# Attention and routed experts on one core: the rows of the first and last pair of batches turned by VectorE in squares of 32 instead of by TensorE

## The chip, the cores and the metric

The kernel runs on one core of one Trainium2 chip. The metric is the device time of one execution in microseconds. A core has TensorE (PE; its weight loads are shown apart as PEld), VectorE (DVE), ScalarE (ACT), GpSimd (POOL) and SyncE (SP), each with its own queue of instructions in program order, and 16 DMA engines that all queues share.

## The reference

Two blocks, one behind the other. First attention with a linear bias, a causal window of 128 and a softmax; then a gate picks one of eight experts for each token, and the token's row goes through that expert's two matrices and is scaled by the gate's probability.

```python
# q, k, v: (8 batches, 8 heads, 576 positions, 64), float32
scores = q @ k.T / sqrt(64)
rel = pos[:, None] - pos[None, :]
scores = where((rel >= 0) & (rel < 128), scores - slope[h] * abs(rel), -1e9)
x = softmax(scores) @ v               # -> rows of tokens: (4608, 512)

logits = x @ w_gate                   # (4608, 8)
expert = argmax(logits, 1)
gate = softmax(logits)[expert]
y = relu(x @ w1[expert]) @ w2[expert] # w1: (8, 512, 1024), w2: (8, 1024, 512)
out = gate[:, None] * y
```

## The kernel before

**Attention.** Batches are taken in four pairs (`bp` 0 to 3), and a pair in four units of two heads (`u` 0 to 15). A unit is worked in four steps, so a loop of 64 iterations (`i = 4 * u + g`) carries the attention. In iteration i TensorE makes the scores of iteration i+2 (`scores`, L756), ACT takes their exponential (L762), VectorE multiplies them by the bias factors (L765, L770), and TensorE multiplies the probabilities of iteration i by the values (`values`, L791). `finish` copies the sum of a half unit to `xT` by ACT, adds up the softmax's denominators by TensorE (L823) and adds them to `sumT` by VectorE (L834). So `xT` holds the attention's result of a pair with features on partitions and tokens along the columns, not yet divided.

**Loads.** SP issues them: `load_part` in iteration i loads a quarter of unit u+2, the keys at g = 0, the queries at g = 1, the values of one batch at g = 2 and of the other at g = 3. Ahead of each stands a copy of four bytes, `no_earlier_than` (L636), that waits for the multiplied probabilities of iteration i+1. The values of units 6 and 7 are the exception: POOL issues those, and nothing holds them back but their buffer, of which there are three. In units 5 and 6 SP also loads quarters of the first expert's first matrix (L561).

**Rows.** When a pair is done, its rows must go to the DRAM tensor `x_rows`, token by token, so that the experts can gather them. A pair has nine tiles of 128 tokens (`t` 0 to 8; tile 8 holds 64 tokens of each batch). `row_turned` turns a tile by four TensorE transposes into a PSUM tile `m` (L1007), and ACT copies it to a tile `xs` (L1009). `row_out` has POOL put the row's scales `es` into the last columns (L1016) and store the row by one DMA (L1021). A row in `x_rows` is four pieces of 132 numbers: 32 features of each of four head pairs, and four scales. There are four `xs` tiles in turn (pool `rows`), and two PSUM tiles `m`, which the row transposes share with `finish`, `gate`, `turn`, `place` and `enlist`.

**Order of the work behind a pair.** The order is written by hand. For each pair the gate's logits (`gate`, `turn`), the scales (`scale_a`, `scale_b`, `scale_c`; the last gives `es`), the place of each token in its expert's list (`count`, `place`, `ones_at`, `enlist`) and the nine rows are cut into tasks. `behind(bp)` lists 16 for pairs 0 and 1, and one is taken at the end of each iteration of the next pair (at g = 2 in its middle). For pair 0 these are iterations 16 to 31; rows 0 and 1 are turned in iterations 21 and 23, `scale_c`, `count` and the first two stores lie in iteration 24, and rows 2 to 8 in iterations 25, 26, 27, 29, 30 and 31. Pair 3 has no attention behind it: `with_tail` lists 14 tasks, and `strassen1` of the first expert takes one after each of its 14 groups of matmuls.

**Experts.** An expert's first 512 tokens go through both layers with seven half-size products instead of eight (`strassen1`, L1357; `strassen2`, L1414); the sums that this needs are VectorE's (L529 to L532 and L537 to L540). Tokens beyond 512 go through small plain groups (L1453, L1469). The first two experts gather whole rows, which TensorE turns (L1177); all others gather by pieces into squares of 32, which VectorE turns (`to_columns`, L1180). The constant `to_squares` holds four 0/1 matrices that carry a number per token to the place where its squares lie; `pieces` uses it for the indices (L1056). The second expert's weights take the memory of the pools that hold `xT` and `xs`, so their load waits until those are done with (`end_of_tail`).

Of the kernel before, what the change touches and what calls it, by code (L numbers as in the profile page):

```python
# [8 lines left out]
F32 = mybir.dt.float32  # L9
# [6 lines left out]
P = 128  # L16
# [441 lines left out]
def kernel(  # L458
# [12 lines left out]
    nc = tc.nc  # L471
# [8 lines left out]
    HP = H // 2  # L480
    KB = P // 2
# [24 lines left out]
    with ExitStack() as fast:  # L506
# [99 lines left out]
        def load_v(u, b, eng, k0=0, k1=NK):  # L606
            bp, hp = units[u]
            if u not in v_sb:
                v_sb[u] = vp.tile([P, NK, P], F32, name="v_sb")
            eng.dma_start(  # L610
                v_sb[u][b * KB : (b + 1) * KB, k0:k1, :], v4[2 * bp + b, :, k0:k1, hp * P : (hp + 1) * P],
            )
# [391 lines left out]
        def row_turned(bp, t):  # L1004
            ps = ps_m.tile([P, 512], F32, name="m")
            for hp in range(HP):
                nc.tensor.transpose(ps[:, hp * P : (hp + 1) * P], xT[bp][:, hp, t * P : (t + 1) * P], ident[:])  # L1007
            xs = xs_of[bp, t] = rows.tile([P, NA, PW], F32, name="xs")
            nc.scalar.copy(  # L1009
                xs[:, :, :PD].rearrange("p a (h f) -> p h a f", h=HP), ps.rearrange("p (h a f) -> p h a f", h=HP, a=NA),  # L1010
            )

        def row_out(bp, t):

            xs = xs_of.pop((bp, t))
            nc.gpsimd.tensor_copy(  # L1016
                xs[:, :, PD:].rearrange("p (r x) h -> p r x h", r=2),
                es_of[bp][:, t].unsqueeze(2).to_broadcast([P, 2, 2, HP]),
            )
            for p0, n, r0 in placed(bp, t):  # L1020
                nc.gpsimd.dma_start(x_d[r0 : r0 + n, :], xs[p0 : p0 + n].rearrange("p a w -> p (a w)"))  # L1021

        def row(bp, t):
            row_turned(bp, t)
            row_out(bp, t)


        NC = E * NJ + XU
        g_idx = rte.tile([P, NR * NJ], I32, name="g_idx")
        p_idx = rte.tile([P, NC - NR * NJ, NA], I32, name="p_idx")  # L1030
# [479 lines left out]
        def with_tail(g, w2s):  # L1510

            bp = BP - 1
            rs = [lambda t=t: row(bp, t) for t in range(TPB)]
            early = [lambda t=t: row_turned(bp, t) for t in range(3)]
            w = [[f] for f in w2s]
            a, b, c, n, p, o, e = (
                [lambda f=f: f(bp)] for f in (scale_a, scale_b, scale_c, count, place, ones_at, enlist)
            )
# [81 lines left out]
```

## Time and profile before

| | us |
|---|---|
| median of 3 runs | 687.96 |
| the three runs | 686.35, 687.96, 689.75 |
| the profiled execution | 687.13 |
| its span, first to last instruction | 685.4 |
| TensorE busy in it | 663.6 |
| VectorE, ACT, POOL busy | 366.9, 208.3, 229.8 |
| attention, about | 0 to 177 |
| first expert's first layer with pair 3's tasks, about | 177 to 213 |
| all other experts' work, about | 213 to 685 |

The page gives busy times for each engine, and a chain: the work that ended last, followed back from the last instruction. A group of instructions is one line: line of the kernel, engine, operation, tile written and tiles read, shape, count, then busy time and the mean time of one in ns, then the engine's idle time just before them and what ended it. Views by stretch give the busy time of every engine between two moments, the clock granted to TensorE (1.00 is full speed) and the DMA engines' share. All times are microseconds from the span's start.

### The profile page before, as it was taken

The page shows a single profiled execution, that of the slowest core. Times are in us where ns is not written, and L with a number is a line of the kernel's source. Part 1 is how long each engine was busy: PE and PEld are TensorE (multiplying, and loading weights), DVE is VectorE, ACT ScalarE, POOL GpSimd, SP SyncE. Part 2 cuts the span into 40 slices and gives each one's busy share as a digit, 9 for nine tenths or more (in the row PEclk, how much of TensorE's full clock was granted, in tenths as well). Part 3 has the DMA queues.
Part 4 walks back from the last instruction along what each step waited for, and adds up shares of the span by engine and source line. Part 5 has one row for each costly group of instructions (what it writes and reads, how often), then busy time and mean ns, then how long its engine had stood idle before and what let it go on. Part 6 is the DMA issues. An engine that isn't in the chain of part 4 may idle for free.

```text
span 685.4 us, 14622 instructions
## 1 busy us (share of the span) xinstructions
PE 663.6 (97%) x6096; PEld 557.5 (81%) x6096; DVE 366.9 (54%) x691; ACT 208.3 (30%) x379; POOL 229.8 (34%) x344
## 2 busy tenths in 40 slices
PE   7998998999999999999999999999999999999996
PEld 6877877787688888878897887888788878878893
DVE  4556749786469467614843563385157435633500
ACT  5655555465342223113112310231131123012210
POOL 8010412215033175217224702752272257023020
PEclk9999999999999999999999999999999999999998
DMA  8776978875428555284457328542834583294010
GB/s 261 207 207 194 296 239 241 231 236 168 138 96 318 186 185 166 62 295 143 148 183 279 85 99 290 187 163 82 298 123 142 180 280 100 80 303 158 1 61 9
DMA packets 56909, 122.00 MB, mean 178 GB/s; under 512 B 5345, under 2 KB 22529, under 8 KB 56834
## 3 DMA queue, kind: packets, MB, share of 16 engines
q1 hardware_dynamic: 44562, 89.17, 40.3%
q0 software_dynamic: 11120, 30.92, 13.6%
q8 instruction: 50, 0.82, 0.5%
q10 hardware_dynamic: 1152, 0.88, 0.4%
q14 instruction: 25, 0.20, 0.1%
HBM read 101.79 MB, written 19.96 MB: 178 GB/s over the span
## 4 chain that ended last, share of the span: by engine, by line
PE 83%; issue 9%; DVE 4%; ACT 2%; POOL 1%; DMA 1%; ACTq 0%; POOLq 0%; DVEq 0%
PE sp L756 6%; PE at L791 5%; PE pair0b L1357 5%; PE pair1b L1414 5%; PE pair1a L1414 5%; PE pair0a L1357 4%; PE pair2b L1357 4%; PE pair0a L1414 4%; PE pair2a L1357 4%; PE pair0b L1414 4%; PE pair1b L1357 4%; PE pair2a L1414 4%; PE pair1a L1357 4%; PE pair2b L1414 4%; PE m L823 3%
## 5 line engine op out<-in xcount | busy, mean ns | idle before, releaser
L1152 POOL DMA_INDIRECT xg<-x_rows,p_idx x124 | 124.8, 1006 | 37.8 <-issue 36.9
L1437 POOL DMA_INDIRECT out_dram<-zo,s_idx x39 | 44.7, 1146 | 249.7 <-DVE zo L1428 133.4
L765 DVE TENSOR_TENSOR pe<-pe,fac 128x768 f32<-128x768 f32 x48 | 45.9, 959 | 40.2 <-ACT pe L762 40.0
L756 PE MATMUL sp<-q_sb,k_sb 64*64 64x192 f32 (+2 forms) x1152 | 59.1, 326 | 8.4 <-DMA q_sb<-in_qT_dram 4.9
L762 ACT ACTIVATE pe<-sp 128x768 f32<-128x768 f32 x64 | 51.9, 811 | 43.0 <-PE sp L756 40.4
L791 PE MATMUL at<-pe,v_sb 64*64 64x192 f32 (+2 forms) x1408 | 59.8, 290 | 0.9 <-DVE pe L765 0.7
L756 PEld LDWEIGHTS sp<-q_sb,k_sb 64*64 64x64 f32 x1152 | 42.0, 139 | 17.5 <-issue 7.3
L791 PEld LDWEIGHTS at<-pe,v_sb 64*64 64x64 f32 x1408 | 47.4, 138 | 7.1 <-issue 2.3
L1016 POOL COPY xs<-es 128x16 f32<-128x16 f32 x36 | 11.3, 314 | 82.4 <-DVE es L930 77.4
L1021 POOL DMA_DIRECT2D x_rows<-xs x40 | 21.9, 549 | 35.6 <-issue 16.3
L1368 ACT ACTIVATE h<-h 128x512 f32<-128x512 f32 x32 | 20.2, 632 | 39.5 <-DVE h L1367 39.5
L823 PE MATMUL m<-pe,ind 128*32 128x192 f32 (+2 forms) x704 | 29.5, 286 | 0.3 <-issue 0.3
L1009 ACT COPY xs<-m 128x512 f32<-128x512 f32 x36 | 20.7, 585 | 22.4 <-PE m L1007 8.0
L1164 DVE TENSOR_TENSOR xn<-xg 128x512 f32<-128x512 f32 x39 | 26.3, 676 | 0.2 <-DMA xg<-x_rows,p_idx 0.2
L823 PEld LDWEIGHTS m<-pe,ind 128*32 128x32 f32 x704 | 23.0, 109 | 2.7 <-issue 0.7
L1007 PE MATMUL m<-ident,xT 128*128 128x128 f32 x144 | 21.8, 282 | 2.1 <-DVE sumT L834 1.7
L1180 DVE STREAM_TRANSPOSE xgT<-xn 128x512 f32<-128x512 f32 x31 | 22.1, 711 | 1.1
L537 DVE TENSOR_TENSOR w2s<-w 128x512 f32<-128x512 f32 x16 | 11.0, 688 | 20.0 <-DMA w<-in_moe_w_dram 20.0
L1469 PE MATMUL pair2a<-w,h 128*128 128x512 f32 x48 | 21.1, 592 | 0.0
L1007 PEld LDWEIGHTS m<-ident,xT 128*128 128x128 f32 x144 | 15.8, 142 | 5.9 <-DVE sumT L834 2.1
L808 ACT COPY xT<-at 128x640 f32<-128x640 f32 (+1 forms) x32 | 18.7, 585 | 5.7 <-PE at L791 5.6
L770 DVE TENSOR_TENSOR pe<-pe,fac 128x768 f32<-128x768 f32 x16 | 15.3, 954 | 8.8 <-ACT pe L762 8.8
(364 smaller groups left out, 1384.8 us busy)
## 6 DMA issues: line engine op xcount, KB each, us to landing
w<-in_moe_w_dram SPq DMA_DIRECT2D x29, 2048.0 KB
k_sb<-in_kT_dram SPq DMA_DIRECT2D x15, 576.0 KB
q_sb<-in_qT_dram SPq DMA_DIRECT2D x15, 576.0 KB
x_rows<-xs POOLq DMA_DIRECT2D x32, 264.0 KB, 4.5
v_sb<-in_v_dram SPq DMA_DIRECT2D x26, 288.0 KB
w<-in_moe_w_dram SPq DMA_DIRECT2D x4, 512.0 KB
xg<-x_rows,p_idx POOLq DMA_INDIRECT x124, 2.6
v_sb<-in_v_dram POOLq DMA_DIRECT2D x4, 288.0 KB, 7.7
```

Source lines behind the costliest of these rows:

```text
L756: nc.tensor.matmul(sp[c * KB : (c + 1) * KB, r, c0 : c0 + n], lhsT=k_sb[u][hs, c, kb * KB : (kb + 1) * KB], rhs=q_sb[u][hs, c, kb * KB : k ...
L762: nc.scalar.activation(pe[:], sp[:, :, :GC], AF.Exp, scale=SCALE)
L765: nc.vector.tensor_tensor(pe.rearrange("p r (k c) -> p r k c", k=2), pe.rearrange("p r (k c) -> p r k c", k=2), fac[:, h0 : h0 + 2, None, ...
L791: nc.tensor.matmul(acc[r * D : (r + 1) * D, c, lo - q0 : hi - q0], lhsT=v_sb[u][c * KB : (c + 1) * KB, kb, r * D : (r + 1) * D], rhs=pe[c ...
L823: nc.tensor.matmul(sm[32 * j : 32 * j + 32, lo - q0 : hi - q0], lhsT=none[:] if pe is None else ind[:, hp, :], rhs=fac[:, 0, :KB] if pe is ...
L1007: nc.tensor.transpose(ps[:, hp * P : (hp + 1) * P], xT[bp][:, hp, t * P : (t + 1) * P], ident[:])
L1152: nc.gpsimd.indirect_dma_start(out=to, out_offset=None, in_=where, in_offset=bass.IndirectOffsetOnAxis(ap=idx, axis=0),)
L1164: nc.vector.tensor_tensor(xn[:], x, s.unsqueeze(3).to_broadcast([P, NA, HP, TQ]), op=ALU.mult)
L1180: nc.vector.transpose(to.rearrange("p h (k j) -> p k h j", j=TQ), xn[:])
L1357: nc.tensor.matmul(ps[:, f * 256 : (f + 1) * 256], lhsT=left[m][:, d, fb * P : (fb + 1) * P], rhs=right[m][:, d, :], start=(m in (1, 2, 5) ...
L1414: nc.tensor.matmul(ps[:, :256], lhsT=left[m][:, f, c * P : (c + 1) * P], rhs=right[m][:, f, :], start=(m in (1, 2, 5) and f == 0), stop=Tr ...
L1437: ins = nc.gpsimd.indirect_dma_start(out=out[:, :], out_offset=bass.IndirectOffsetOnAxis(ap=s_idx[:, g["c0"] + j : g["c0"] + j + 1], axis= ...
```

## The change

For pairs 0 and 3 the rows are no longer turned by TensorE. VectorE turns each 32x32 square of `xT` in place of its tile (`squares_turned`), so that in `xs` partition 32a + i holds piece a of the tokens i, 32 + i, 64 + i and 96 + i. The scales must lie on those partitions too: `scales_squared` carries `es` there by four products with `to_squares` and two ACT copies. `squares_out` puts them in by POOL and stores by pieces: one DMA for each of the four pieces (eight for tile 8), in runs of 132 numbers. Pair 0 stores from POOL, tile by tile. Pair 3 turns its tiles 0 to 7 into a spare `xT` buffer, and SP stores them in groups of four tiles, then tile 8. The rows of pairs 1 and 2 stay as they were. The values of units 6 and 7 are issued by SP like all others.

```diff
-                load_v(u, g - 2, nc.gpsimd if u in (6, 7) else nc.sync)
+                load_v(u, g - 2, nc.sync)
...
+        def scales_squared(bp):
+            ps = ps_m.tile([P, 512], F32, name="m")
+            n = TPB * H
+            for k in range(NA):
+                nc.tensor.matmul(
+                    ps[:, k * n : (k + 1) * n], lhsT=K["to_squares"][:, k, :],
+                    rhs=es_of[bp].rearrange("p t r h -> p (t r h)"), start=(k == 0), stop=True, skip_group_check=True,
+                )
+            sq = sq_of[bp] = small.tile([P, TPB, NA, HP], F32, name="sq")
+            ps5 = ps[:, : NA * n].rearrange("p (k t r h) -> p k t r h", k=NA, t=TPB, r=2)
+            for r in range(2):
+                half = slice(r * KB, (r + 1) * KB)
+                nc.scalar.copy(sq[half].rearrange("p t k h -> p k t h"), ps5[half, :, :, r, :])
+
+        def squares_turned(bp, t):
+            if bp in spare and t < TPB - 1:
+                w = NA * PW
+                flat = spare[bp].rearrange("p h n -> p (h n)")
+                xs = flat[:, t * w : (t + 1) * w].rearrange("p (k w) -> p k w", k=NA)
+            else:
+                xs = rows.tile([P, NA, PW], F32, name="xs")
+            xs_of[bp, t] = xs
+            nc.vector.transpose(
+                xs[:, :, :PD].rearrange("p k (h j) -> p k h j", h=HP),
+                xT[bp][:, :, t * P : (t + 1) * P].rearrange("p h (k i) -> p k h i", k=NA),
+            )
+
+        def squares_out(bp, t, eng, n=1):
+            for k in range(t, t + n):
+                nc.gpsimd.tensor_copy(xs_of[bp, k][:, :, PD:], sq_of[bp][:, k])
...
+            for p0, m, r0 in placed(bp, t):
+                for a in range(NA):
+                    eng.dma_start(
+                        x_d[r0 : r0 + n * m, a * PW : (a + 1) * PW].rearrange("(k i) w -> i k w", i=TQ),
+                        xs[a * TQ : (a + 1) * TQ, p0 // TQ : p0 // TQ + n * m // TQ, :],
+                    )
...
 # behind(bp)
+            if bp == 0:
+                turned = [lambda t=t: squares_turned(bp, t) for t in range(2)]
+                outs = [lambda: scales_squared(bp)] + [lambda t=t: squares_out(bp, t, nc.gpsimd) for t in range(2)]
+                rs = [
+                    lambda t=t: (squares_turned(bp, t), squares_out(bp, t, nc.gpsimd)) for t in range(TPB)
+                ]
             return [g3[0:1], g3[1:2], g3[2:] + t3[0:1], t3[1:], a, turned[0:1], b, turned[1:2], c + n + outs,
                     rs[2:3], p + rs[3:4], rs[4:5], o, rs[5:6], rs[6:7], e + rs[7:9]]
...
 # with_tail(g, w2s)
-                [lambda k=k: gate(bp, k) for k in range(3)], [lambda k=k: turn(bp, k) for k in range(3)], a, early[0:2], b,
-                early[2:3] + w[0], c + n + [lambda t=t: row_out(bp, t) for t in range(3)], rs[3:5] + w[1],
-                p + rs[5:6], rs[6:7], o, rs[7:9] + w[2], e + w[3] + w[4], [table_fixed] + w[5],
+                [lambda k=k: gate(bp, k) for k in range(3)] + rt[0:1], [lambda k=k: turn(bp, k) for k in range(3)] + rt[1:2],
+                a, rt[2:3], b, rt[3:4], c + n, rt[4:5] + w[0], q + p + ro[0:1] + rt[8:9], rt[5:6] + o, rt[6:8] + ro[2:3],
+                e + ro[1:2] + w[1], [table_fixed] + w[2], w[3] + w[4] + w[5],
```

In `with_tail`, `rt` are the nine turns, `ro` the three groups of stores, `q` is `scales_squared`, and `w` are the first expert's `w2` sums.

More of the change, by code (lines that the diff above doesn't have):

```diff
@@ L1025, in row @@
             row_out(bp, t)
+        sq_of = {}
+        spare = {}
+        def scales_squared(bp):
[26 more added lines that the diff above has]
+                nc.gpsimd.tensor_copy(xs_of[bp, k][:, :, PD:], sq_of[bp][:, k])
+            if n == 1:
+                xs = xs_of.pop((bp, t))
+            else:
+                w = NA * PW
+                flat = spare[bp].rearrange("p h n -> p (h n)")
+                xs = flat[:, t * w : (t + n) * w].rearrange("p (k w) -> p k w", k=n * NA)
+            for p0, m, r0 in placed(bp, t):
[4 more added lines that the diff above has]
+                    )
         NC = E * NJ + XU
@@ L1512, in with_tail @@
             bp = BP - 1
-            rs = [lambda t=t: row(bp, t) for t in range(TPB)]
-            early = [lambda t=t: row_turned(bp, t) for t in range(3)]
+            spare[bp] = xp.tile([P, HP, 2 * S], F32, name="xT")
+            rt = [lambda t=t: squares_turned(bp, t) for t in range(TPB)]
+            ro = [lambda: squares_out(bp, 0, nc.sync, 4), lambda: squares_out(bp, 4, nc.sync, 4), lambda: squares_out(bp, 8, nc.sync)]
             w = [[f] for f in w2s]
-            a, b, c, n, p, o, e = (
-                [lambda f=f: f(bp)] for f in (scale_a, scale_b, scale_c, count, place, ones_at, enlist)
+            a, b, c, n, q, p, o, e = (
+                [lambda f=f: f(bp)]
+                for f in (scale_a, scale_b, scale_c, count, scales_squared, place, ones_at, enlist)
             )
             todo = [
-                [lambda k=k: gate(bp, k) for k in range(3)], [lambda k=k: turn(bp, k) for k in range(3)], a, early[0:2], b,
-                early[2:3] + w[0], c + n + [lambda t=t: row_out(bp, t) for t in range(3)], rs[3:5] + w[1],
-                p + rs[5:6], rs[6:7], o, rs[7:9] + w[2], e + w[3] + w[4], [table_fixed] + w[5],
+                [lambda k=k: gate(bp, k) for k in range(3)] + rt[0:1], [lambda k=k: turn(bp, k) for k in range(3)] + rt[1:2],
+                a, rt[2:3], b, rt[3:4], c + n, rt[4:5] + w[0], q + p + ro[0:1] + rt[8:9], rt[5:6] + o, rt[6:8] + ro[2:3],
+                e + ro[1:2] + w[1], [table_fixed] + w[2], w[3] + w[4] + w[5],
             ]
```

## Prediction

> **What bounds the kernel now.** First the page's busy row, its clock row and its chain, to see which engine to count in.
>
> ```profile
> PE 663.6 (97%) x6096; PEld 557.5 (81%) x6096; DVE 366.9 (54%) x691; ACT 208.3 (30%) x379; POOL 229.8 (34%) x344
> PEclk9999999999999999999999999999999999999998
> PE 83%; issue 9%; DVE 4%; ACT 2%; POOL 1%; DMA 1%; ACTq 0%; POOLq 0%; DVEq 0%
> ```
>
> TensorE is busy for 97% of the span and is 83% of the chain, so work taken from it counts, unless another engine becomes late in that stage. Next the groups of instructions, for what a row costs.
>
> ```profile
> L1007 PE MATMUL m<-ident,xT 128*128 128x128 f32 x144 | 21.8, 282 | 2.1 <-DVE sumT L834 1.7 <-ACT xs L1009 0.4
> L1009 ACT COPY xs<-m 128x512 f32<-128x512 f32 x36 | 20.7, 585 | 22.4 <-PE m L1007 8.0 <-issue 7.1 <-POOL xs L1016 6.1
> L1180 DVE STREAM_TRANSPOSE xgT<-xn 128x512 f32<-128x512 f32 x31 | 22.1, 711 | 1.1
> L1021 POOL DMA_DIRECT2D x_rows<-xs x40 | 21.9, 549 | 35.6 <-issue 16.3 <-ACT xs L1009 12.5 <-POOL xs L1016 6.9
> L1056 PE MATMUL m<-ta,to_squares 128*128 128x24 f32 (+1 forms) x16 | 1.9, 252 | 0.0
> DMA to landing us min/median/max: 2.3/4.6/8.2
> ```
>
> (The last line is from the question about L1021: issue of a row store to its landing.) Then the busy times by stretch; columns are PE, PEld, DVE, ACT, POOL, granted clock, DMA share, GB/s.
>
> ```profile
> 52.40:56.90 4.50, 4.48 (x109) 3.75 (x108) 2.58 (x10) 3.39 (x6) 0.23 (x1) 1.00 0.88 223
> 56.90:60.30 3.40, 0.80 (x25) 0.83 (x29) 3.26 (x9) 0.02 (x1) 0.00 (x0) 1.00 0.24 74
> 60.30:63.70 3.40, 3.40 (x60) 3.36 (x56) 1.90 (x6) 1.54 (x2) 0.00 (x0) 0.50 0.69 193
> 65.00:95.00 30.00, 29.10 (x608) 22.98 (x610) 17.95 (x36) 16.50 (x28) 8.84 (x19) 1.00 0.87 279
> 177.20:213.00 35.80, 34.54 (x206) 28.80 (x205) 22.83 (x59) 14.15 (x27) 7.85 (x19) 1.00 0.44 156
> ```
>
> Last the timeline where TensorE stands still in the first pair's stage.
>
> ```profile
> 51.13 0.37 SPq L598 DMA_DIRECT2D q_sb<-in_qT_dram  x1
> 51.17 1.46 POOL L610 DMA_DIRECT2D v_sb<-in_v_dram  x2 [9.21 <-PE at L791]
> 59.50 0.72 PE L756 MATMUL sp<-q_sb,k_sb 64*64 64x192 f32 x12 [2.63 <-issue]
> ```
>
> The reader is to see one event here. Unit 6's queries (L598) and unit 7's values, which POOL issues as soon as their buffer is free, leave within 0.04 us and share the DMA engines. The queries land only at 59.4 (8.3 us; the keys just before, issued at 48.80, took 4.6), the scores of unit 6 wait 2.63 us, and the clock is half for the 3.41 us from 60.28: 2.6 + 1.7 = 4.3 us lost.
>
> **The change, part by part.** "Iteration" is a step of the attention loop, four to a unit; pair 0's row work lies in iterations 20 to 31 (52 to 88 us), pair 3's between 177 and 213.
>
> *Values of units 6, 7 to SyncE.* Four loads move behind SP's pace copies: unit 7's are issued in iterations 22 and 23 rather than at 51.17. SP's other value loads take 0.67 us of issue each, and SP is two units ahead. The queries of unit 6 then land in the 4.6 us of the keys, by about 54, before they are asked for at 56.9. The 4.3 us go. What is late next is VectorE, below.
>
> *Rows of pair 0.* Removed: 9 rows of four transposes, 0.58 us each by start to start on TensorE (74.64 to 75.22 in one row): 5.2 us, and 9 ACT copies of 0.585, which cost nothing beside 16.5 of 30 us busy. Added on VectorE: 9 transposes of the L1180 kind and size, 9 x 0.71 = 6.4 us. Added on TensorE: four products with `to_squares`, 8 instructions; L1056 has 16 in 1.9 us, so 1.0 us (72 columns against 24 is no dearer: L993's 18 with 48 columns take 2.14). ACT gets two small copies, about 0.3 us each, between its exponential of 72 elements (L924, 0.26) and its copy of 256 (L832, 0.37).
>
> The price is a wait. In the old order `es`, the last result of VectorE's scale chain, was read by POOL alone; now TensorE reads it in `scales_squared` at the end of iteration 24, and iteration 25's scores are queued behind. I laid the stage out by hand, each engine in program order with the trace's durations; done for the old kernel it puts iteration 32 at 87.0 us (trace: 87.6). For the new one, without the query wait, TensorE begins iteration 24 at 60.1 instead of 65.3. VectorE has been full since 55.05 (`scale_a`, multiplication 23, transpose 0, a sum, `scale_b`), so multiplication 24 ends at 62.2: TensorE idle 1.5. Multiplications 25 and 26, a sum, transpose 1 and four small operations bring `es` at 65.7: idle 2.7. Iteration 32 starts at 84.5. The account for pair 0: 4.3 + 5.2 won; 1.0 for products, 4.2 for the two waits, 0.8 for a half clock after them, some 1.0 for smaller waits on VectorE paid: 2.5 us won.
>
> *Clock, rule against row.* The Trainium skill (TensorE: Matmul & The Clock Gate, Part 1) lets the clock fall after an idle window of about 3.4 us and asks for no gaps over about 3 us. Here 2.63 us were enough, as the second and third stretch above show (1.00, then 0.50). By the rule waits of 1.5 and 2.7 us cost no clock and the pair wins 3.3; by the row they do. I take the row, and keep 0.8 for the range.
>
> *Transposes, rule against row.* The skill's VectorE: DVE Perf Modes, The three transpose paths and the rules after it, sends a 128x128 transpose to TensorE and gives VectorE 311 ns for one in bf16. A row holds four, an estimate of 1.24 us: 4.8 us more VectorE time a pair, which would undo either stage's gain. L1180 does the same operation on the same 128x512 f32 in 0.71, from SBUF to SBUF too; the row decides.
>
> *Stores of pair 0.* POOL issues 40 DMAs instead of 10, 0.55 us each, so a row takes 0.2 + 0.3 + 4 x 0.55 = 2.7 us of POOL; nothing else is queued on POOL there once the values are gone. But the `xs` tiles are four: transpose t waits for row t-4 to land, and VectorE's next multiplication stands behind it. POOL also has eight completion semaphores in turn, so a row's stores follow the landing of those two rows earlier. The landing of a 66 KB piece isn't in the trace; whole rows of 264 KB took 3.8 to 8.2 us in this stage, about 5.5 at the median. Lower end: 2.3, the trace's minimum, no wait at all; upper end 8.2. At 5.5 only row 8 waits, 0.8 us, unfelt by TensorE. Each us above 5.5 costs about 2.5 to 3 (rows 4, 6 and 8 wait in turn). I take 5.5, the median of the nearest row.
>
> *Rows of pair 3.* They lie among the first expert's products, where TensorE is full (34.5 of 35.8 us). Removed: 36 transposes, 4.9 us there. Added: products 1.0. VectorE goes from 22.8 to 29.2 of some 33 us: nearly full. Its queue delays the one-hot operations (`ones_at`, 2.5 us), and the `enlist` products wait for them: about 1.0 idle where before 0.6 was, and smaller delays of 0.7. Won: 4.9 - 1.0 - 1.0 - 0.7 = 2.2. The order of the weight sums also changes; the second layer's first use of one (213.0 + 7.4 = 220.4) keeps 1 to 2 us of slack.
>
> *Stores of pair 3.* Ten DMAs of POOL become 16 on SP, in front of the next expert's weight loads (issued at 206.92 and 207.35, landed at 216.1 and 221.7). These must now wait until the spare `xT` tile has been stored, about 213, and would land by 228. They are first needed at 240: hidden, with 12 us to spare; without that cover it would be the 6 us of delay. The gather for that expert waits for the last rows either way: before, issue 211.43, landing 217.74, gather 218.58; now about 214 to 218. The columns needed from it are made at 228.9.
>
> *Sum.* 2.5 + 2.2 = 4.7. The profiled execution took 687.13 us (span 685.4), which gives 682.4; the median of the three runs, 687.96, lies 0.83 higher: 683.2.
>
> **Rivals.** *Stores land late (ends slower).* Place: transposes 4, 6 and 8 of pair 0 waiting for `xs`. For: DMA share 0.87 there, four times the DMAs, 528-byte runs instead of 2112. Against: same bytes, and the values' load is moved to a stretch with share 0.24. At 7.4 us of landing the win is gone (688); at 8.5 it gives 691.7, from there on slower. *VectorE fills pair 3's stage*: any further delay reaches the adds that TensorE's accumulators wait for, and the 2.2 are lost: 685.4. *The query wait is no part of a usual execution*: then pair 0 without it pays 1.7 net (my schedule of the old kernel without the wait ends 4.2 earlier), and 687.96 + 1.7 - 2.2 = 687.5. *No half clock and early landings*: 683.2 - 0.8 - 1.5, the second for the smaller waits: 680.9.
>
> **How the numbers follow.** The forecast, 683.2, has 0.48, with a range of its own from 681.5 to 684.5; the better case 0.08; VectorE full 0.08; no usual query wait 0.10; late stores that only eat the gain 0.09; late stores that make it slower 0.17. A measurement of this kernel tells about 0.5% from no change, so 684.5 to 691.4 is "same": faster 0.56, same 0.27, slower 0.17. The range runs from 679.5 to 690.0; about 0.17 lies above, 0.03 below.
>
> **What would show it.** Right: no 2.6 us gap before L756 at 57; a gap before the products of `scales_squared` near 64, put down to VectorE's `es`; a half clock near 67; STREAM_TRANSPOSE of `xs` 18 times at about 0.71; the first expert's second layer (L1414) beginning near 208.3 instead of 213.0. Wrong: multiplications idle on a DMA of `x_rows` near 75 to 92, or `pair` matmuls after 177 with gaps put down to DVE.

## The result and the profile after

| | before | after |
|---|---|---|
| median of 14 runs each, us | 688.03 | 687.16 |
| the profiled execution, us | 687.13 | 685.88 |
| its span, us | 685.4 | 683.7 |

The ratio of the times is 0.9981, 95% interval 0.9962 to 1.0000: 0 to 2.6 us, about 1.3, where 4.7 were forecast, and less than a measurement of this kernel can tell.

The page of after, in the order shown for before: busy row, granted clock, chain.

```profile
PE 657.9 (96%) x6040; PEld 551.5 (81%) x6040; DVE 377.0 (55%) x709; ACT 200.0 (29%) x365; POOL 236.7 (35%) x360
PEclk9998999999999999999999999999999999999998
PE 66%; issue 17%; DVE 6%; POOL 5%; DMA 3%; ACT 1%; POOLq 0%; ACTq 0%; DVEq 0%
```

The groups of the rows' lines:

```profile
L1007 PE MATMUL m<-ident,xT 128*128 128x128 f32 x72 | 11.2, 284 | 1.7 <-DVE sumT L834 1.3 <-ACT xs L1009 0.4
L1054 DVE STREAM_TRANSPOSE xs<-xT 128x512 f32<-128x512 f32 x10 | 7.0, 705 | 2.0 <-DMA x_rows<-xs 1.9
L1071 POOL DMA_DIRECT2D x_rows<-xs x40 | 21.7, 548 | 6.8 <-DMA x_rows<-xs 2.8 <-POOL xs L1062 2.2 <-DVE sumT L834 1.2
```

and, in the answer on L1071, the landing of a stored piece:

```profile
DMA to landing us min/median/max: 3.3/5.1/6.5
```

TensorE has lost 5.7 us of work, and half of the transposes are gone; but its share of the chain fell from 83% to 66%, and one slice of the clock row shows 8. Where is that? The timeline of TensorE in the first pair's stage:

```profile
56.20 0.88 PE L756 MATMUL sp<-q_sb,k_sb 64*64 64x192 f32 x16
...
63.06 0.88 PE L791 MATMUL at<-pe,v_sb 64*64 64x192 f32 x16 [2.10 <-DVE pe L765]
...
66.47 1.95 PE L1036 MATMUL m<-es,to_squares 128*128 128x72 f32 x8 [2.53 <-DVE es L930]
```

The scores of iteration 24 start at 56.20 (59.50 before) with no wait for queries. The two waits that the forecast put at 1.5 and 2.7 us are there, with 2.10 and 2.53. Then the stretches; columns are PE, PEld, DVE, ACT, POOL, granted clock, DMA share, GB/s:

```profile
57.95:61.36 3.41, 2.93 (x76) 2.03 (x68) 3.17 (x10) 1.80 (x5) 0.00 (x0) 1.00 0.84 266
61.36:64.77 3.41, 0.88 (x16) 0.56 (x16) 3.34 (x8) 0.64 (x2) 0.00 (x0) 1.00 0.84 270
64.77:68.18 3.41, 1.71 (x8) 1.74 (x8) 1.67 (x6) 0.00 (x0) 0.00 (x0) 0.50 0.83 257
68.18:71.60 3.42, 3.42 (x60) 2.88 (x63) 0.73 (x1) 1.70 (x4) 2.13 (x5) 0.50 0.75 214
177.20:210.30 33.10, 31.49 (x178) 25.95 (x177) 26.54 (x68) 10.24 (x20) 1.34 (x9) 1.00 0.36 103
```

The clock is half for 6.82 us, not for 3.41. VectorE is full while TensorE waits (3.34 of 3.41). The last row is the pair 3 stage, 33.1 us instead of 35.8.

The whole difference can be laid out by stretches. The marks are starts of TensorE's instructions: first scores of iteration 23, first scores of iteration 36, first product of the first expert, its second layer (L1414, now L1469), the 29th group of products, the last product group, and the end. An iteration is named here by its scores, which TensorE makes two loop steps earlier: the start that the forecast calls iteration 32 is the first score of iteration 34. The piece from the 29th group (241.20 before) to the last (671.78) takes 430.57 us in both.

| stretch, us | before | after | forecast | measured |
|---|---|---|---|---|
| to iteration 23 | 53.73 | 53.57 | 0 | -0.16 |
| S: iterations 23 to 36, pair 0's rows | 41.02 | 40.34 | -2.5 | -0.68 |
| to the first expert, pairs 1 and 2 | 82.56 | 83.31 | 0 | +0.75 |
| T: to its second layer, pair 3's rows | 35.74 | 33.08 | -2.2 with U | -2.66 |
| U: to the 29th group | 28.16 | 29.06 | | +0.90 |
| experts | 430.57 | 430.57 | 0 | 0 |
| rest | 13.59 | 13.77 | 0 | +0.18 |
| sum | 685.37 | 683.70 | -4.7 | -1.67 |

S gave too little; T and U together gave 1.76, near their 2.2. The experiments ask why. Some of their runs fell on chips where every kernel, the one before too, took 6 to 8% longer (in the experts' part of their traces TensorE waited 24 to 32 us and its clock was half for 31 to 41 us; why stays open), so of those runs only S, T, U and the closing are read, and a ratio is always to before on the same chip.

### The profile page after: what moved, and what is told of

Same layout as the page of the kernel before. It is cut to its first block, busy times and chain, and to the rows that moved or that the text cites. A ratio compares the mean times of both kernels' runs of the same rounds, so it can differ in the third digit from the quotient of the medians.

```text
span 683.7 us, 14553 instructions
## 1 busy us (share of the span) xinstructions
PE 657.9 (96%) x6040; PEld 551.5 (81%) x6040; DVE 377.0 (55%) x709; ACT 200.0 (29%) x365; POOL 236.7 (35%) x360
## 4 chain that ended last, share of the span: by engine, by line
PE 66%; issue 17%; DVE 6%; POOL 5%; DMA 3%; ACT 1%; POOLq 0%; ACTq 0%; DVEq 0%
PE pair0b L1412 4%; PE pair0a L1412 4%; PE pair1b L1469 4%; PE pair1a L1469 4%; PE pair1b L1412 4%; PE pair2b L1412 4%; PE pair0b L1469 4%; PE pair0a L1469 4%; PE pair1a L1412 4%; PE pair2a L1412 4%; PE pair2a L1469 4%; PE pair2b L1469 4%; PE pair1a L1524 2%; PE pair0a L1524 2%; PE pair2a L1524 2%
## 5 line engine op out<-in xcount | busy, mean ns | idle before, releaser
L791 PE MATMUL at<-pe,v_sb 64*64 64x192 f32 (+2 forms) x1408 | 59.8, 286 | 4.1 <-DVE pe L765 2.8
L791 PEld LDWEIGHTS at<-pe,v_sb 64*64 64x64 f32 x1408 | 47.0, 136 | 11.5 <-issue 5.2
L756 PEld LDWEIGHTS sp<-q_sb,k_sb 64*64 64x64 f32 x1152 | 41.6, 138 | 13.9 <-DMA q_sb<-in_qT_dram 4.1
L1071 POOL DMA_DIRECT2D x_rows<-xs x40 | 21.7, 548 | 6.8 <-DMA x_rows<-xs 2.8
L1062 POOL COPY xs<-sq 128x16 f32<-128x16 f32 x10 | 3.0, 304 | 50.4 <-ACT sq L1044 50.4
L1412 PE MATMUL pair0b<-xgT,w 128*128 128x256 f32 x72 | 17.2, 382 | 0.0
L1412 PE MATMUL pair0a<-xgT,w 128*128 128x256 f32 x72 | 17.0, 379 | 0.0
L1469 PE MATMUL pair1b<-w,h 128*128 128x256 f32 x72 | 17.0, 379 | 0.0
```

What stands on the lines that cost most here:

```text
L756: nc.tensor.matmul(sp[c * KB : (c + 1) * KB, r, c0 : c0 + n], lhsT=k_sb[u][hs, c, kb * KB : (kb + 1) * KB], rhs=q_sb[u][hs, c, kb * KB : k ...
L791: nc.tensor.matmul(acc[r * D : (r + 1) * D, c, lo - q0 : hi - q0], lhsT=v_sb[u][c * KB : (c + 1) * KB, kb, r * D : (r + 1) * D], rhs=pe[c ...
L1412: nc.tensor.matmul(ps[:, f * 256 : (f + 1) * 256], lhsT=left[m][:, d, fb * P : (fb + 1) * P], rhs=right[m][:, d, :], start=(m in (1, 2, 5) ...
L1469: nc.tensor.matmul(ps[:, :256], lhsT=left[m][:, f, c * P : (c + 1) * P], rhs=right[m][:, f, :], start=(m in (1, 2, 5) and f == 0), stop=Tr ...
```

## The experiments

All are edits of the changed kernel. The table has S, T and U as above, the time from POOL's last scatter to the end of the span (closing), and the ratio of the times to before with its interval; "d" marks a disturbed chip.

| run | S | T | U | closing | ratio |
|---|---|---|---|---|---|
| before | 41.02 | 35.74 | 28.16 | 5.67 | 1 |
| after | 40.34 | 33.08 | 29.06 | 5.84 | 0.9981 (0.9962 to 1.0000) |
| v_only, d | 36.94 | 35.74 | 28.16 | 14.77 | 1.0074 (1.0021 to 1.0127) |
| v_only_b | 38.52 | 35.73 | 28.16 | 14.92 | 1.0077 (1.0050 to 1.0104) |
| p0_only, d | 43.29 | 35.74 | 28.16 | 8.47 | 1.0064 (1.0030 to 1.0097) |
| p3_only, d | none | 33.08 | 28.90 | 15.48 | 1.0188 (1.0116 to 1.0261) |
| v_p3, d | 36.94 | 33.08 | 28.79 | 13.91 | 1.0090 (1.0048 to 1.0131) |
| v_p3_b | 37.93 | 33.08 | 28.95 | 13.85 | 1.0025 (1.0006 to 1.0044) |
| v_p3_t8 | 36.93 | 33.08 | 28.72 | 14.37 | 1.0038 (1.0015 to 1.0060) |
| v_p3_pieces, d | 39.21 | 34.77 | 28.16 | 5.84 | 0.9984 (0.9953 to 1.0015) |
| v_p3_pieces_b | 38.87 | 33.09 | 28.88 | 5.85 | 0.9932 (0.9902 to 0.9961) |
| es_late | 41.15 | 33.08 | 28.99 | 5.95 | 0.9980 (0.9954 to 1.0007) |
| es_late_b5, d | 38.25 | 34.76 | 28.16 | 5.87 | 0.9994 (0.9959 to 1.0028) |
| es_late_b5_b | 37.06 | 34.76 | 28.16 | 5.86 | 0.9964 (0.9940 to 0.9988) |
| sq_late_b5, d | 38.42 | 33.08 | 29.10 | 5.87 | 0.9954 (0.9922 to 0.9986) |
| sq_late_r8 | 38.42 | 34.77 | 28.16 | 5.82 | 0.9934 (0.9908 to 0.9959) |
| pieces_o, d | 38.25 | 32.49 | 29.54 | 5.94 | 0.9956 (0.9909 to 1.0004) |
| sq_late_o, d | 39.85 | 32.50 | 31.30 | 5.83 | 0.9926 (0.9880 to 0.9972) |

### The parts by themselves: v_only, p0_only, p3_only, v_p3

```diff
 # v_only and v_p3: pair 0 as before
-            if bp == 0:
+            if False:
 # p0_only and p3_only: values as before
-                load_v(u, g - 2, nc.sync)
+                load_v(u, g - 2, nc.gpsimd if u in (6, 7) else nc.sync)
 # v_only and p0_only: the old with_tail; p3_only: pair 0 as before too
```

> Only the four value loads of units 6 and 7 go to SyncE; all rows stay as before. My theory (the wait for unit 6's queries is in every execution of before, and costs 2.6 us of idle and 1.7 of half clock): no gap at L756 near 57, iteration 32 earlier by about 4.2 us, and most of it kept to the end: 3.5 to 4.3 us faster than before, ratio about 0.994. Rival A (the query wait is no part of a usual execution): within 1 us of before. Rival B (what is won in the first pair's stage is given back in the pairs between, whatever it was): iteration 32 earlier by about 4 but the second expert's start earlier by less than 2.

> Only the first pair's rows are turned in squares; values of units 6, 7 stay on POOL and the last pair's rows stay as before. The trace of after shows two waits of TensorE on VectorE (2.1 and 2.5 us) and half clock for 6.83 us. My theory: with the query wait still there VectorE is no longer late (the scores wait 2.6 us and VectorE catches up), so the waits on VectorE shrink below 1.5 us in all, the 5.2 us of transposes go and 1.0 of products come: 1 to 3 us faster than before. Rival (the rows cost what the hand schedule gives without the query wait, whatever the values do): 1.7 to 2.9 us slower.

> Only the last pair's rows are turned in squares; values and the first pair stay as before. My theory from the trace of after: 2.4 us won until the second layer of the first expert begins (near 210.6 instead of 213.0), of which 0.9 is given back because the next expert's gather leaves no earlier than before (218.5) and its columns wait: 1.5 us faster than before, ratio 0.998. Rival (the gather is late by chance of that execution): 2.4 us faster. Rival (VectorE fills the stage and the win is an accident of its state on entry): within 0.5 us.

> Values by SyncE and the last pair in squares; the first pair's rows stay with TensorE and ACT as before. If the two add: 3.5 to 4.3 from the values and 1.5 from the last pair, 5.0 to 5.8 us faster than before (about 682.5), and 4 us faster than the full change: then the first pair's squares are the part that eats the gain. If the query wait is no part of a usual execution: 1.5 faster (686.5), and the first pair's squares are neutral.

The stage answers. With the values alone S is 4.08 us shorter: the step was right (4.3). TensorE in v_only, at the scores of iteration 24 and behind multiplication 24:

```profile
55.88 0.88 PE L756 MATMUL sp<-q_sb,k_sb 64*64 64x192 f32 x16
...
61.71 0.56 PE L791 MATMUL at<-pe,v_sb 64*64 64x192 f32 x8 [0.79 <-DVE pe L765]
```

With TensorE turning the rows, VectorE is 0.79 us late at multiplication 24 instead of 2.10. With the squares alone S is 2.27 us longer than before, where 1 to 3 us shorter was expected. TensorE in p0_only:

```profile
60.08 0.88 PE L756 MATMUL sp<-q_sb,k_sb 64*64 64x192 f32 x16 [3.50 <-issue]
...
69.02 1.08 PE L1036 MATMUL m<-es,to_squares 128*128 128x72 f32 x8 [2.23 <-DVE es L930]
...
81.56 0.37 PE L791 MATMUL at<-pe,v_sb 64*64 64x64 f32 x8 [2.23 <-DVE pe L765]
```

The expectation was right at one place: behind the query wait VectorE did catch up, and the wait at multiplication 24 (2.10 in after) is gone. But the wait for `es` stayed, and the third line is another wait, behind the fifth row's transpose, which itself started 1.76 us late with no releaser in the profile. The clock was half for 3.41 us twice, from 61.27 and from 81.75. So the squares cost pair 0's stage 2.3 us beside the query wait (0.9 of it is the query wait itself, 3.50 against 2.63), and 3.4 without it (after's S less v_only's). In p3_only the late query load came already at iteration 20, so S has no meaning there; T is 33.08, as in after, and U gives 0.74 back. The two right parts together, v_p3, have S and T of both. Yet by their ratios all these kernels were 0.6 to 1.9% slower than the one before, which ran on the same chip.

### Two of them again, on another chip: v_only_b, v_p3_b

> Only the values of units 6, 7 by SyncE, as in the first trial of it; wanted is its median, which that trial could not give[...]. Its trace gained 4.1 us between iterations 23 and 36. My theory (the query wait is in every execution of before): 3.5 to 4.5 us faster than before (ratio 0.994). Rival (it is in some executions only): less than 2 us faster, with a wide spread of before.

> The full change without the first pair's squares. Stage readings so far: values 4.1, last pair 2.65 until the first expert's second layer begins and 0.6 to 0.9 given back in it. If these add: 5.5 to 6.2 us faster than before (ratio 0.9915), so the first pair's squares cost the full change about 4 to 5 us at the median. Rival (what the two gain is covered by a later wait): no more than 2 us faster, like the full change.

The ratios stayed above 1, though TensorE's last product group began at 669.70 and 666.03 (before 671.78, after 669.93). The forecast of the times failed and that of the stages held, but for a query load that came late near 78 in both runs (1.47 and 0.76 us), hence S of 38.5 and 37.9. What follows the products is longer. Each kernel's span, and POOL's last scatter in its timeline, in before:

```profile
core 0: 685.4 us, clock 0.995
679.71 1.00 POOL L1437 DMA_INDIRECT out_dram<-zo,s_idx  x1 [13.24 <-ACT zo L1475]
```

in after:

```profile
core 0: 683.7 us, clock 0.992
677.86 0.98 POOL L1492 DMA_INDIRECT out_dram<-zo,s_idx  x1 [13.23 <-ACT zo L1530]
```

and in v_p3_b:

```profile
core 0: 687.8 us, clock 0.992
673.96 0.98 POOL L1492 DMA_INDIRECT out_dram<-zo,s_idx  x1 [13.24 <-ACT zo L1530]
```

That is 5.7, 5.8 and 13.9 us from the start of the scatter to the end. The page does not count what lies there as busy; the trace's records of POOL show two instructions there that stand in no line of the kernel, INC_SWDGE_SEM and DRAIN:

```text
kernel                  POOL DMAs   INC_SWDGE_SEM ns   DRAIN ns
before                  217          500               1295
after                   233          536               1458
p0_only                 247         1060               3582
v_p3, v_p3_b            203         2115               7910
v_p3_t8                 211         2195               8237
v_only, v_only_b        213         2295               8645
p3_only                 207         2435               9217
```

The two executions of v_only, on different chips, agree to the ns. The pairs lie within 20 ns of a line (DRAIN = 4.09 x INC_SWDGE_SEM - 752 ns), but not in the order of the number of DMAs.

### The closing held equal: v_p3_pieces

```diff
 # row_out, pair 0 turned by TensorE as before
-                nc.gpsimd.dma_start(x_d[r0 : r0 + n, :], xs[p0 : p0 + n].rearrange("p a w -> p (a w)"))
+                for a in range(NA):
+                    nc.gpsimd.dma_start(x_d[r0 : r0 + n, a * PW : (a + 1) * PW], xs[p0 : p0 + n, a])
```

> The full change without the first pair's squares, whose rows are turned by TensorE and ACT as before, but stored by POOL in four pieces each, so that POOL issues the same DMAs in the same order as in the full change. In the run without squares TensorE's last products began at 666.0 (full change 669.9, before 671.8), yet its span was longer than before: POOL's last two instructions, the closing INC_SWDGE_SEM and DRAIN, took 2.1 and 7.9 us there, 0.54 and 1.46 in the full change. My theory (these two depend on the list of POOL's DMAs alone): 0.5 and 1.5 us here, the last products near 666, and 681 to 682 us, 5.5 to 7 us faster than before: then the first pair's squares cost the full change 5 us. Rival A (the closing time is tied to the row stage itself, or to when POOL's last DMA leaves): again 8 us, and about 690. Rival B (the pieces themselves cost the first pair's stage something): iteration 36 later than 91.3 by over 1 us.

> The full change without the first pair's squares, rows turned by TensorE and ACT and stored in four pieces each: wanted is its median where the experts' part is not disturbed. The closing INC_SWDGE_SEM and DRAIN took 0.54 and 1.46 us in its first trace, as in the full change; the first pair's stage won 1.8 to 2.5 us. My theory: last products near 667, 681.5 to 683 us, 5 to 6 us faster than before. Rival (the gain of the part kernels was not real, the closing time only moved it): within 1.5 us of the full change, 686 or more.

The same number of POOL DMAs as after has, and the closing is that of after: 540 and 1458 ns, in both runs. Rival A fell: the row stage is v_p3's, the closing isn't. On the quiet chip the ratio is 0.9932, 4.7 us faster than before (5 to 6 were expected), and the span 680.3. So the full change without pair 0's squares wins as much as was forecast for all of it, and the two ratios put the price of the squares at 0.0049 of 688, 3.4 us (with their intervals about 1 to 6). That this is also the 3.4 of S is chance: in the two spans, 3.4 us apart too, 1.5 lie in S, 1.2 in pairs 1 and 2 and the rest elsewhere. Rival B was right: stored in pieces, the stage loses some 2 us of v_p3's (S 38.87 against 36.94).

### The wait for es moved away: es_late

```diff
-    ... a, turned[0:1], b, turned[1:2], c + n + outs, rs[2:3], ...
+    ... a, turned[0:1], b, turned[1:2], c + n, outs + rs[2:3], ...     # pair 0
```

> The full change, with the products of the scales and the first two rows' stores one iteration later (iteration 25 instead of 24). My theory (the mis-sized term is the wait for es plus the second window of half clock that it brings): no gap above 0.5 us before L1036, half clock for one window or none, iteration 34 earlier by 2.5 to 4.5 us than in the full change (81.9 to 83.9), and 2.5 to 4 us faster than it: about 683.5. Rival A (VectorE is simply full, and what it does not keep TensorE waiting for at es it will a multiplication later): the wait moves to L791 and at most 1 us is won. Rival B (the stores leave 2 us later, the transposes wait for their tiles): waits on x_rows grow from 1.9 to over 5 us, and nothing is won.

My theory of one mis-sized wait fell here. The timeline of TensorE in es_late:

```profile
63.34 0.88 PE L791 MATMUL at<-pe,v_sb 64*64 64x192 f32 x16 [2.09 <-DVE pe L765]
...
66.75 1.08 PE L1036 MATMUL m<-es,to_squares 128*128 128x72 f32 x8 [1.33 <-DVE es L930]
...
79.59 0.49 PE L791 MATMUL at<-pe,v_sb 64*64 64x64 f32 x8 [4.02 <-DVE pe L765]
```

and on VectorE, ahead of the third line:

```profile
77.98 0.71 DVE L1054 STREAM_TRANSPOSE xs<-xT 128x512 f32<-128x512 f32 x1 [4.00 <-DMA x_rows<-xs]
```

The wait for `es` shrank and the clock stayed up behind it, but the fifth row's transpose then waited 4.00 us for the first row's stores to land, with a multiplication and TensorE behind it. The clock fell there instead, for one stretch (the columns are those of the stretches above):

```profile
75.82:79.23 3.41, 0.00 (x0) 0.00 (x0) 1.25 (x2) 0.08 (x1) 1.64 (x3) 1.00 0.95 239
79.23:82.64 3.41, 3.05 (x44) 2.41 (x48) 3.38 (x5) 0.69 (x1) 3.12 (x6) 0.50 0.99 290
```

S is 0.8 longer than after's. Rival B named the right place, but not the cause: the first store did not leave later, it left at 69.1 (69.7 in after). The transposes came earlier. In after the fifth transpose started at 77.2, just behind the landing of the first row's last piece at 76.9; in es_late VectorE was ready for it at 74.0, and that piece landed at 77.9. So in after the transposes waited for stores for only 0.16 and 1.75 us, the 1.9 of the L1054 group: the stop at `es` and the half clock had given the stores the time. One wait covers the other.

### One more row tile, and later transposes: es_late_b5, sq_late_b5, sq_late_r8

```diff
-        rows = pool(tail, "rows", 4, side="right")
+        rows = pool(tail, "rows", 5, side="right")          # all three
 # sq_late_b5, pair 0: transposes 0 and 1 go with the products, in iteration 25
+    [g3.., t3.., a, [], b, [], c + n, turned + outs, p + rs[2:3], rs[3:5], o, rs[5:6], rs[6:7], e + rs[7:9]]
 # sq_late_r8: as sq_late_b5, with rs[8] in iteration 33
```

> The full change with the products of the scales one iteration later, and five row tiles instead of four. With four, the wait for es shrank from 2.5 to 1.3 us, but the fifth row's transpose then waited 4.0 us for the first row's stores to land and TensorE 4.0 behind it. My theory (the first pair's stage is a chain: scales, POOL's stores at 3 us a row, landing, the tile, VectorE; what one link is given another takes as long as the tiles are four): the wait on x_rows falls below 1.5 us, no wait of TensorE above 2.2, no half clock, iteration 34 near 83 to 84.5 and 682 to 684 us. Rival (VectorE is full, 30 of 40 us in the stage, and holds TensorE up whatever the tiles): iteration 34 after 86, no gain over the full change.

> The full change with the products of the scales one iteration later and five row tiles, again for its median. In its first trace iteration 36 came 2.8 us earlier than before (full change 0.7), and with the last pair's 1.9 that makes 4.7: 682.5 to 684 us, 3 to 4 us faster than the full change. Rival (given back in the pairs between): 685.5 or more.

> As the last, with the first two transposes moved too, from iterations 21 and 23 to iteration 25, behind multiplication 24 and the scales. My theory (the 2.1 us of wait at multiplication 24 are 0.8 of the scale chain, as in the run with the values alone, and 1.4 of the two transposes ahead of it): the first wait falls to 0.8, and iteration 34 comes 0.5 to 1.3 us earlier than in the last run. Rival (what leaves there is missing later, since the rows start later on POOL): waits on x_rows of 2 us and more, iteration 34 no earlier.

> As the run with the first two transposes moved to iteration 25, and with the ninth row's transpose two iterations later, in iteration 33. That run had iteration 34 5.7 us earlier than before, and lost 3.1 of it by iteration 36: the ninth transpose waited 3.8 us for the fourth row's stores, a multiplication stood behind it, TensorE 1.5 us behind that, and the clock was half for 3.4 us. My theory (that wait is the last link of the chain): no wait on x_rows over 1 us, no half clock in the stage, iteration 36 earlier by 5 to 5.7 us, and with the last pair's 1.9 some 680 to 681.5 us, the fastest of all. Rival (the wait comes back elsewhere, at the fifth to eighth row): iteration 36 earlier by less than 4 us, and 682.5 or more.

With the fifth tile S falls from 41.15 to 38.25 and 37.06, and the ratio to 0.9964 on the quiet chip. The rival "VectorE is full, whatever the tiles" fell; the half clock, expected to go, came once in each of the two executions. In sq_late_b5 the wait at multiplication 24 fell only to 1.50 (0.8 was expected), yet iteration 34 came 5.73 us earlier than before (after 1.03), counted from iteration 23. The last link then showed, on VectorE:

```profile
86.66 0.71 DVE L1054 STREAM_TRANSPOSE xs<-xT 128x512 f32<-128x512 f32 x1 [3.78 <-DMA x_rows<-xs]
```

and behind it on TensorE:

```profile
88.27 0.34 PE L791 MATMUL at<-pe,v_sb 64*64 64x64 f32 x8 [1.53 <-DVE pe L765]
```

With the ninth row two iterations later (sq_late_r8) no transpose waits for a store. S did not gain in that execution: a query load came late, as in v_only_b, and the clock fell for 3.41 us there and again in T. TensorE in sq_late_r8:

```profile
62.88 0.88 PE L791 MATMUL at<-pe,v_sb 64*64 64x192 f32 x16 [1.50 <-DVE pe L765]
...
65.70 0.52 PE L1036 MATMUL m<-es,to_squares 128*128 128x72 f32 x3 [0.74 <-DVE es L930]
...
77.80 0.60 PE L756 MATMUL sp<-q_sb,k_sb 64*64 64x192 f32 x4 [1.51 <-DMA q_sb<-in_qT_dram]
```

Its ratio, 0.9934, is near that of the kernel without the squares (0.9932, rows in pieces). Freed of their chain of waits, the squares of pair 0 neither cost nor win anything that these ratios, each known to about 2 us, could tell. The expected 680 to 681.5 was missed (683.63, within the rival's 682.5 or more, though the rows waited for no store).

### What pair 3 gives back: v_p3_t8, pieces_o, sq_late_o

```diff
 # v_p3_t8: tile 8 stored by POOL, behind the second block
-  lambda: squares_out(bp, 8, nc.sync)]        ... rt[6:8] + ro[2:3], e + ro[1:2] + w[1]
+  lambda: squares_out(bp, 8, nc.gpsimd)]      ... rt[6:8], e + ro[1:3] + w[1]
 # pieces_o, sq_late_o (on v_p3_pieces and sq_late_r8)
-  rt[5:6] + o, rt[6:8]
+  o + rt[5:6], rt[6:8]
```

> The full change without the first pair's squares, and with the ninth tile of the last pair stored by POOL behind the second block's copies, so that SyncE's second block of stores does not stand behind eight DMAs. My theory (the gather for the second expert waits for SyncE's late stores): that block is issued from about 207 instead of 210, the gather leaves 2 to 4 us earlier than 218.5, the wait of 2.6 us on xg goes to under 0.5, the 0.6 to 0.9 us given back in the first expert's second layer are kept: 0.5 to 0.9 us faster than without this step. Rival (the give-back is VectorE's queue, not the gather): the same within 0.3 us. Rival (POOL's own DMAs hold the gather up): slower by up to 2 us.

> The change without the first pair's squares, stores in pieces (0.9932 of before in its last run), with the last pair's one-hot operations (ones_at) ahead of the sixth transpose on VectorE instead of behind it. My theory: the enlist products wait for gsr, which stands behind that transpose; the wait of 0.97 us at L993 falls to 0.3, the stretch of idle and thin products after it no longer halves the clock in any execution (it did in two of the traces, 1.9 us each): 0.5 to 1.5 us faster, ratio 0.991 to 0.993. Rival (VectorE only shifts the wait to the next sum): the wait moves to another line, no gain.

> The change with the later squares of the first pair (five row tiles, transposes from iteration 25, the ninth in 33; 0.9934 in its last run), with the same turn of order in the last pair. My theory: its last trace lost 1.9 us to half clock behind the enlist products and 1.5 us to a late query load at L756; the first goes here, the second is chance: 681.5 to 683, ratio 0.990 to 0.992. Rival: as above, the same 0.9934.

The gather for the second expert was one suspect for U. In v_p3_t8 its last part left 5.9 us earlier than in v_p3_b. POOL's timeline in v_p3_t8:

```profile
213.04 1.46 POOL L1201 DMA_INDIRECT xg<-x_rows,g_idx  x1 [0.30 <-issue]
```

and in v_p3_b:

```profile
218.90 0.94 POOL L1201 DMA_INDIRECT xg<-x_rows,g_idx  x1 [0.30 <-issue]
```

and U still gave back 0.56 instead of 0.79: the gather is the smaller part. The rest fits the rival, VectorE's queue. The only wait of TensorE over 0.15 us that the profile has in U is one on VectorE's `tb`, 0.32 us in v_p3_t8 and 0.55 in v_p3_b. VectorE was busy for 18.45 us in U before and 20.13 in after: some of its work of T has moved there. With the one-hot operations first, the wait at L993 fell from 0.97 to 0.38 (pieces_o, TensorE) and T by 0.59:

```profile
207.57 0.65 PE L993 MATMUL m<-oc,gsr 128*128 128x48 f32 x4 [0.38 <-DVE gsr L983]
```

but U took it back (28.88 to 29.54). Both runs fell on a disturbed chip, so these two U and their ratios don't settle it. In sq_late_r8 the half clock in T cost TensorE 1.7 us, VectorE did 28.15 us of work in T instead of 26.54, and U was 28.16, as before, with nothing given back. That speaks for a backlog of VectorE; no run takes the backlog away by itself, so it is argued and not shown.

## Why the prediction was wrong

**Values of units 6, 7: right.** 4.3 forecast, 4.08 in three traces. In two others another query load was late by 0.76 and 1.47 us: what the move wins is not safe from the next collision. The rival that the wait is no part of a usual execution fell: the trace of v_only shows it gone and p0_only shows it there, 3.50 us long; p3_only, where POOL issues these values too, has a late query load of 2.62 us at iteration 20.

**Rows of pair 0: the failed step.** The sum for the squares was 5.2 won against 1.0 + 4.2 + 0.8 + 1.0 paid, a loss of 1.8; measured 3.4 (S against v_only's). The products (eight of L1036 in 1.08 us at full clock) and the transposes (0.70 us each, the nearest row's 0.71) had the right size, and the two waits nearly so, 4.6 against 4.2. The mis-sized term is the half clock. For it 0.8 was put in, about what one stretch of 3.41 us costs when TensorE works in half of it. The clock was half for two such stretches: in the first (64.77 to 68.18) TensorE was busy for 1.71 us at half speed, 0.85 of work lost, in the second for 3.42, 1.71 lost. That is 2.6 us, 1.8 more than was put in. The busy times over the whole of S, in v_only and in after, close the account:

```profile
52.81:89.75 36.94, 35.58 (x788) 28.84 (x777) 26.46 (x60) 20.89 (x35) 8.96 (x19) 1.00 0.86 277
53.57:93.91 40.34, 34.67 (x760) 27.88 (x749) 31.59 (x69) 16.69 (x28) 20.22 (x41) 0.92 0.85 255
```

Without the 2.6 lost to the clock, TensorE's work in after is 32.1 us, 3.5 less than in v_only, where 5.2 - 1.0 = 4.2 was forecast. It is idle for 5.7 us against 1.4, 4.3 more, where 4.2 + 1.0 = 5.2 was forecast. These two misses, 0.7 and 0.9, nearly cancel each other; the half clock is what is left. The rule that the forecast set against the row of the transposes is one for a whole 128x128, which squares of 32 are not, and its estimate of 1.24 us for a row did not hold.

**But the term could not have been won back by itself.** es_late took away both stretches of half clock behind `es` and half of that wait, and won nothing: a wait of 4.02 us and another stretch of half clock came in their place. The forecast took the stores as free up to a landing of 5.5 us, "only row 8 waits, 0.8 us" (rows counted from 0). The landing was 5.1 at the median, as assumed; but a row took POOL 2.7 to 3.9 us, start to start, where 2.7 was the sum, and the first row's stores left at 69.7, late behind `es` at half clock. Once the stop at `es` is shorter, row 4 waits (es_late), and with the fifth tile row 8 (sq_late_b5). The rival "stores land late" had the right mechanism, hidden in after by the wait that the forecast did see. The two were counted as separate terms, and they are links of one chain: scales, POOL, landing, tile, transpose, multiplication, TensorE.

**Pairs 1 and 2: 0.75 paid, none forecast.** Around the scores of iteration 47 TensorE waited 0.80 us with no releaser in the profile, and for as long in v_only_b and es_late_b5_b, but not in before. Four quiet traces without that wait (v_p3_b, v_p3_t8, v_p3_pieces_b, sq_late_r8) took 82.0 to 82.1 us for this stretch, 0.5 less than before. What the wait is stays open.

**Rows of pair 3: near, in part by luck.** 2.2 forecast for the stage and nothing after it; T gave 2.66 and U took 0.90, two misses that offset each other. The L993 wait was 0.97 (forecast 1.0). VectorE had 26.5 us of work in T, not the 29.2 of the forecast. "Hidden, 12 us to spare" held for the weights, but not, it seems, for VectorE's queue.

**From profile to median.** 0.83 was added; after's median lies 1.28 over its profile. The profiled executions differ by 1.25 us and the medians by 0.87.

**Clock, rule and row.** The Trainium skill (TensorE: Matmul & The Clock Gate, Part 1) has a free-running window of 3413 ns; every fall ahead of the second expert lasted one or two steps of 3.41 us, which agrees. It lets the clock fall after an idle window (its rule of no gaps over about 3 us stands in the section Why this matters for your kernels). In after TensorE was busy for 0.88 us of the 3.41 ahead of the first stretch, and for 1.71 of the first stretch itself, which a second followed. es_late_b5_b shows two more falls, each as the window ahead and the one at half clock; the last line is a window of after that was followed by full clock:

```profile
60.20:63.61 3.41, 1.31 (x28) 0.97 (x32) 3.17 (x9) 0.96 (x2) 0.00 (x0) 1.00 0.91 297
63.61:67.03 3.42, 3.42 (x54) 3.09 (x46) 3.32 (x10) 0.81 (x1) 0.00 (x0) 0.50 0.73 217
200.15:203.56 3.41, 2.44 (x20) 2.01 (x18) 3.41 (x6) 0.63 (x1) 0.00 (x0) 1.00 0.91 203
203.56:206.97 3.41, 3.41 (x12) 2.87 (x12) 3.14 (x7) 0.63 (x1) 0.00 (x0) 0.50 0.39 98
201.30:204.72 3.42, 2.46 (x12) 1.80 (x10) 3.39 (x6) 0.63 (x1) 0.00 (x0) 1.00 0.87 183
```

The same wait of 2.1 us at L791 brought the clock down in es_late_b5_b, where one window held all of it, and not in es_late, where two windows shared it (2.08 us busy in one of them). And the same wait of 0.97 us at L993 brought it down where its window also held most of the `enlist` products of 48 columns (the third line), and not in after, where the window ended with the wait and held wide products alone (the last line): thin products seem to count for little. Busy time alone does not decide: 2.44 and 2.46 us here, and a window with 2.08 us, 72-column products among them, brought the clock down in es_late_b5. The runs show the cases, not the threshold. So the half clock is partly a draw of where the window lies, and a forecast should give it a chance and not a fixed part.

## What to carry to other kernels

A wait that one step brings can be the cover of another: before a price is put on a buffer or a store, take the stage's known wait out of the schedule and see what is late then. When a part kernel's stages gain and its time does not, lay the span out in stretches that add up, closing included, before a cause is looked for in the stages. Price the half clock beside a wait of TensorE: behind waits of 1 to 2.5 us that one window held, it cost some 1.6 to 2.6 us more.

## What the runs showed of the hardware

- The end of this program changed with the list of its POOL DMAs. INC_SWDGE_SEM and DRAIN took 1.8 to 11.7 us together, the same in both executions of each kernel that was profiled twice. By the cut of v_p3 to 203 DMAs the closing rose by 8.2 us, more than that kernel's gain of 5.7 in the span to TensorE's last group; 30 more DMAs on POOL brought it back. It does not rise with the number of DMAs; what sets it stays open.
- TensorE's clock fell with 0.97 us of idle in a window of 3.41, and in another execution stayed up with as much (above).
- A SyncE load of 576 KB of queries near 78 us kept TensorE waiting for 0.8 to 2.6 us in four executions (v_only_b, v_p3_b, sq_late_r8, sq_late_o), with whole rows and with pieces stored beside it, and for no time in others of the same kernels' traces (v_only, v_p3).
